# Spectral mix kernel: half of the modes' product is added to the stored x @ w_ch of 24 tiles, and the rest comes in pairs of tiles on 64-row quarters of TensorE

## The chip, the cores and the metric

The kernel runs on one core of one Trainium2 chip. The metric is the device time of one launch in microseconds (us), the median of several runs. Inputs and output are float32 in the chip's DRAM.

## The reference

Eight batches `b`, sequence `S` = 576, `DM` = 512 (8 heads of 64). First a sliding-window attention with a linear bias gives `x` (8 x 576 x 512). Then a spectral step keeps `NM` = 64 modes, and a channel product closes it:

```python
X = np.fft.rfft(x, axis=1)
Xr, Xi = np.real(X[:, :64]), np.imag(X[:, :64])
Yr = einsum('bmd,mde->bme', Xr, w_r) - einsum('bmd,mde->bme', Xi, w_i)
Yi = einsum('bmd,mde->bme', Xr, w_i) + einsum('bmd,mde->bme', Xi, w_r)
y = np.fft.irfft(Yr + 1j * Yi, n=576, axis=1)   # the other modes are zero
u = x + y
out = u + np.maximum(u @ w_ch, 0.0)
```

`w_r` and `w_i` are 64 x 512 x 512 each, 134 MB together, and are read once. Everything else is small beside them.

## The kernel before

The work has three stages.

**Attention** (to about 173 us of the span). It fills `x_sb` and `x4`, the tiles of `x`, and meanwhile a first quarter of the rows of the spectral weights is streamed and used.

**Streaming** (about 173 to 396 us). The other three quarters of the rows of `w_r` and `w_i` come through a ring of three buffers (`RING`), 1.5 MB at a time, two modes by `w_r` or by `w_i`. `_pair(g, m, w)` uses one such load in 24 matmuls (line 792), and `_send(g)` then issues the load that takes over its buffer. The loop runs over `i` from 0 to 59 (`NM - 4` = 60 steps), and the last four steps (60 to 63, with `BUSY` = 12 matmuls of filler after a step, line 709) come after it. The load of the last step is issued when step 60 has been used, in two halves. After every eighth mode the sums go to `ZT` (line 801), in four blocks of 16 modes (real and imaginary part: 32 rows each).

Into this loop other work is put, by the step at which it stands in the program:
- `_ft_steps` builds `FT`, the inverse transform, 128 rows of (mode, part) by 576 positions, for four orders of the mode blocks (one for `b % 4` each).
- `_xt` and `_xw(g, n, xT, psum)`: for each of 36 tiles of 128 positions (`g.seq`), `x` is transposed on TensorE and multiplied by `w_ch` (line 839, four matmuls, and one more where `g.way[n]` is "q", which adds `x`). The result is kept in `g.hl[:, n]` as a high and a low bf16 half: two copies on ScalarE (line 843), and two subtractions on VectorE (line 844), alternating. Its PSUM buffers are two.
- `_z_early(g, b, psum)`, for b = 0 to 7 in steps 50 to 57: of three mode blocks that are done, it makes `Z` (the spectrum, transposed to mode rows) and `ZW` (`Z @ w_ch`), 16 + 16 matmuls on 128 x 32 column strips, then one copy on VectorE and one on ScalarE.

At the end of the loop the PSUM buffers of `_xw` and `_z_early` are given to a new pool, `g.fps`, three `mm` and three `y` buffers, and `_known(g, i)` for the first three tiles is put in front of step 60.

**End** (`_finish`). The last mode block goes through `_z_late` (for four batches at a time) and `_z_take(g, b)`, which copies 32 rows of `ZW` and `Z` of one batch. Each of the 36 tiles needs two PSUM sums: `mm` = stored `x @ w_ch` + `FT.T @ ZW`, and `y` = `x` (for "a" tiles) + `FT.T @ Z`. `_halves` makes such a term as two matmuls that stand side by side, 128 rows deep and 64 columns wide each. Then an "a" tile takes ScalarE (relu of `mm`) and VectorE (add `y`), a "q" tile takes VectorE (max of `mm` and `x`), ScalarE (copy of `y`) and GpSimd (add). The store is issued by SyncE. Half of the 36 tiles are "q". The loop of `_finish` issues, for tile `i`, TensorE's work of `i`, the first step of `i - 1`, the add of `i - 2` and the late store of `i - 3`; the order on each engine is the order of the program.

Of the kernel before, what the change touches and what calls it, by code (L numbers as in the profile page):

```python
# [9 lines left out]
FP32 = mybir.dt.float32  # L10
# [6 lines left out]
P = 128  # L17
# [16 lines left out]
def kernel(  # L34
# [64 lines left out]
    g.X[-1] = persist.tile([P, len(GROUPS[-1]), 2, B, NM], BF16, name="Xlast")  # L99

    g.spectra = []
    g.seq = []
    for b in range(B):
        g.seq += [(g.x_sb[:, b, st], ((b, st * P), (b, st * P + 64))) for st in range(4)]
        if b % 2:
            g.seq.append((g.x4[:, b // 2], ((b - 1, 4 * P), (b, 4 * P))))
    g.way = ["q" if 2 <= i < len(g.seq) - 5 and i % 5 in (0, 2, 3) else "a" for i in range(len(g.seq))]

    with tc.manual_schedule(engines={ET.SP, ET.PE, ET.Activation, ET.DVE, ET.Pool}):
        with ExitStack() as wctx:  # L110
# [82 lines left out]
            with ExitStack() as xctx:  # L193
                xt = xctx.enter_context(tc.tile_pool(name="xts", bufs=2))
                xps = xctx.enter_context(
                    tc.tile_pool(name="xps", bufs=2, space=bass.MemoryType.PSUM))
                eps = xctx.enter_context(
                    tc.tile_pool(name="eps", bufs=1, space=bass.MemoryType.PSUM))
                ftq = _ft_steps(g, xt, xps)
                g.Xz = {}  # L200
                _expand(g, 0, xt, xps)
                k, xT = 0, None
                for i in range(NM - 4):
                    m, w = divmod(i, 2)
                    m *= 2
                    _pair(g, m, w)
                    _send(g)
                    if i % MB == 5:
                        _expand(g, m // MB + 1, xt, xps)
                    if i == 2 * RING - 1:  # L210
                        xT = _xt(g, 0, xt, xps)
                    while k < len(g.seq) and k * (NM - 4 - 2 * RING) < (i + 1 - 2 * RING) * len(g.seq):
                        nxt = _xt(g, k + 1, xt, xps) if k + 1 < len(g.seq) else None
                        _xw(g, k, xT, xps)
                        xT, k = nxt, k + 1
                    if i > 2 * RING and ftq:
                        ftq.pop(0)()
                    if 0 <= i - (NM - 14) < B:
                        _z_early(g, i - (NM - 14), eps)
            g.fps = ctx.enter_context(  # L220
                tc.tile_pool(name="fps", bufs=3, space=bass.MemoryType.PSUM))
            g.mm, g.y = {}, {}
            for i in range(3):
                _known(g, i)

            wps = mctx.enter_context(
                tc.tile_pool(name="wps", bufs=1, space=bass.MemoryType.PSUM))
# [82 lines left out]
    g.nc.scalar.activation(g.mask[:, h], g.rel, AF.Exp, scale=-(2.0 ** (-8.0 * (h + 1) / g.H)))  # L310


def _block(c, k):

    return 3 if k == c else c if k == 3 else k


def _ft_steps(g, pool, psum):
# [7 lines left out]
    def begin():  # L326
        box.cvec = pool.tile([P, 1], FP32, tag="cvec", name="cvec", bufs=1)
        nc.vector.memset(box.cvec, 2.0 / S)
        nc.vector.memset(box.cvec[0:1], 1.0 / S)
        nc.vector.memset(box.cvec[64:65], 1.0 / S)  # L330
        box.FTn = pool.tile([P, S], BF16, tag="FTn", name="FTn", bufs=1)
        for c in range(4):
            order = pool.tile([P, P], BF16, tag="order", name="order", bufs=4)
            for k in range(4):
                nc.gpsimd.tensor_copy(
                    order[:, 32 * k : 32 * k + 32].rearrange("p (r m) -> p r m", r=2),
                    src[:, _block(c, k)])
            orders.append(order)

    def natural(st):  # L340
# [489 lines left out]
def _xw(g, n, xT, psum):  # L830


    nc = g.nc
    x = g.seq[n][0]
    xw = psum.tile([P, g.DM], FP32, tag="xw", name="xw")
    if g.way[n] == "q":
        nc.tensor.matmul(xw, lhsT=g.ident_b, rhs=x, start=True, stop=False)
    for dt in range(4):
        nc.tensor.matmul(xw, lhsT=xT[:, dt], rhs=g.wch[:, dt],  # L839
                         start=(dt == 0 and g.way[n] != "q"), stop=(dt == 3))  # L840
    for h in range(2):
        hi, lo = slice(64 * h, 64 * h + 64), slice(64 - 64 * h, 128 - 64 * h)
        nc.scalar.copy(g.hl[hi, n, h], xw[hi])  # L843
        nc.vector.tensor_tensor(  # L844
            out=g.hl[lo, n, h], in0=xw[hi], in1=g.hl[hi, n, h], op=ALU.subtract)


def _z_early(g, b, psum):


    nc = g.nc
    zp = psum.tile([P, 4, P], FP32, tag="zp", name="zp")
    zwp = psum.tile([P, g.DM], FP32, tag="zwp", name="zwp")
    for et in range(4):
        for k in range(4):
            blk = _block(b % 4, k) % 3
            l = g.ZT[:, et, blk, :, b]
            ks = slice(32 * k, 32 * k + 32)
            nc.tensor.matmul(
                zwp[ks], lhsT=l, rhs=g.wch[:, et], start=(et == 0), stop=(et == 3),  # L860
                tile_position=(0, 32 * k))
            nc.tensor.matmul(
                zp[ks, et], lhsT=l, rhs=g.ident_b, start=True, stop=True,
                tile_position=(0, 32 * k))
    nc.vector.tensor_copy(g.Z[:, b], zp.rearrange("p a b -> p (a b)"))
    nc.scalar.copy(g.ZW[:, b], zwp)


def _z_late(g, b0, psum):
# [3 lines left out]
    zp = psum.tile([P, 4, P], FP32, tag="zp", name="zl")  # L873
    for et in range(4):
        for c in range(4):
            l = g.ZT[:, et, 3, :, b0 + c]
            nc.tensor.matmul(
                zwp[32 * c : 32 * c + 32], lhsT=l, rhs=g.wch[:, et],
                start=(et == 0), stop=(et == 3), tile_position=(0, 32 * c))
    for et in range(4):  # L880
        for c in range(4):
            l = g.ZT[:, et, 3, :, b0 + c]
            nc.tensor.matmul(
                zp[32 * c : 32 * c + 32, et], lhsT=l, rhs=g.ident_b, start=True, stop=True,
                tile_position=(0, 32 * c))
# [3 lines left out]
def _z_take(g, b):  # L889
    nc = g.nc  # L890
    zp, zwp = g.late
    ks = slice(32 * (b % 4), 32 * (b % 4) + 32)
    nc.scalar.copy(g.ZW[ks, b], zwp[ks])
    if b % 4 == 2:
        nc.scalar.copy(g.Z[ks, b], zp[ks])
# [1 line left out]
        nc.vector.tensor_copy(g.Z[ks, b], zp[ks])  # L897


def _known(g, i):  # L900

    nc = g.nc
    x = g.seq[i][0]
    g.mm[i] = g.fps.tile([P, g.DM], FP32, tag="mm", name="mm")
    g.y[i] = g.fps.tile([P, g.DM], FP32, tag="y", name="y")
    _halves(nc, g.mm[i], [g.ident2] * 2, [g.hl[:, i, h] for h in range(2)], start=True, stop=False)
    if g.way[i] == "a":
        _halves(nc, g.y[i], [g.ident_b[:, 0:64], g.ident_b[:, 64:128]], [x] * 2,
              start=True, stop=False)


def _finish(g):
# [5 lines left out]
    with ExitStack() as fctx:  # L918
        pool = fctx.enter_context(tc.tile_pool(name="fin", bufs=4))
        lps = fctx.enter_context(  # L920
            tc.tile_pool(name="lps", bufs=1, space=bass.MemoryType.PSUM, side="right"))
        first = [min(i for i, t in enumerate(g.seq) if t[1][0][0] == b and t[1][1][0] == b)
                 for b in range(g.B)]
        _z_late(g, 0, lps)
        _z_take(g, 0)
        o, r, y = {}, {}, {}
# [7 lines left out]

        for i in range(N + 3):
            if i < N:
                if i >= 3:
                    _known(g, i)
                ft = [g.FT[:, b % 4, s : s + 64] for b, s in g.seq[i][1]]
                _halves(nc, g.mm[i], ft, [g.ZW[:, b] for b, _ in g.seq[i][1]],  # L940
                      start=False, stop=True)
                _halves(nc, g.y[i], ft, [g.Z[:, b] for b, _ in g.seq[i][1]],
                      start=(g.way[i] == "q"), stop=True)
            if i == first[3] - 1:
                _z_late(g, 4, lps)
            for b in range(1, g.B):
                if i == first[b] - 3:
                    _z_take(g, b)
            j = i - 1
            if 0 <= j < N:  # L950
# [48 lines left out]
```

## Time and profile before

| what | value |
|---|---|
| median of 3 runs | 436.17 us (435.27 to 436.35) |
| the profiled execution: time, span of its instructions | 434.88 us, 433.1 us |
| mean granted TensorE clock | 0.837 |
| PE, DVE, ACT, POOL busy over the span | 73%, 54%, 49%, 24% |
| DMA rate over the span | 401 GB/s |
| last use of streamed weights starts | 395.22 us |
| first matmul of `_z_late` | 396.08 us |
| last matmuls of the last tile start | 427.09 us |
| last store lands | 432.03 us |

PE is TensorE, DVE is VectorE, ACT is ScalarE, POOL is GpSimd, SP is SyncE. All times in the text are microseconds from the first instruction of the span. An instruction that started at 398.47 and took 0.60 holds its result only at 399.07, but the next one on the same engine can start before that. The profiled execution is one run, 1.29 us below the median, so differences are worked out inside it and then set on the median.

### The profile page before, as it was taken

The numbers are of one execution on the slowest core, as the hardware profiler recorded it, in microseconds if no ns is written. First come the engines' busy times: TensorE is split into PE (matmuls) and PEld (weight loads), VectorE is DVE, ScalarE is ACT, GpSimd is POOL, SyncE is SP. The second block draws the span as 40 slices with busy tenths as digits, with TensorE's granted clock in tenths as the row PEclk, the third lists the DMA queues.
The fourth block names the chain that finished last, engine by engine and source line by source line (L and its number), as shares of the span: only waits on it lengthen the run. The fifth ranks groups of instructions, "written<-read, shape, count | busy, mean of one in ns | idle before, by whom it ended". The sixth has DMA issues, their size and how long they took to land.

```text
span 433.1 us, 11017 instructions
## 1 busy us (share of the span) xinstructions
PE 317.3 (73%) x4684; PEld 206.2 (48%) x4684; DVE 232.8 (54%) x425; ACT 212.4 (49%) x321; POOL 104.3 (24%) x160
## 2 busy tenths in 40 slices
PE   2688888898887787566857657766666579778994
PEld 1466666666666564433434333333333355544552
DVE  6478977777885473143343342433423445512884
ACT  4799969889887650022242322212313234302883
POOL 8766735445444102000000000000000000000983
PEclk9969999999999896557595885556956898989999
DMA  8999999999999999999999999999999999993787
GB/s 289 409 412 414 418 413 396 416 421 415 418 418 422 424 432 426 395 423 433 428 423 434 426 423 431 431 424 432 417 429 432 424 426 426 426 415 128 285 315 275
DMA packets 33664, 173.72 MB, mean 401 GB/s; under 512 B 3792, under 2 KB 3792, under 8 KB 21456
## 3 DMA queue, kind: packets, MB, share of 16 engines
q1 hardware_dynamic: 33616, 173.03, 97.1%
q8 instruction: 36, 0.59, 0.5%
q14 instruction: 12, 0.10, 0.1%
HBM read 163.58 MB, written 9.44 MB: 400 GB/s over the span
## 4 chain that ended last, share of the span: by engine, by line
DMA 58%; PE 22%; ACT 10%; DVE 6%; issue 2%; SPq 0%; ACTq 0%
DMA wring<-in_moe_w_r_dram 30%; DMA wring<-in_moe_w_i_dram 19%; PE acc L792 4%; ACT att L471 4%; DMA hl<-in_k_dram 3%; DMA hl<-in_q_dram 3%; PE mm L826 2%; DMA ZTa<-in_moe_w_r_dram 2%; PE av L496 2%; PE acc L758 2%; PE y L826 2%; PE xw L839 2%; ACT T L423 2%; DVE att L479 2%; DVE hl L844 1%
## 5 line engine op out<-in xcount | busy, mean ns | idle before, releaser
L843 ACT CAST hl<-xw 64x512 bf16<-64x512 f32 x72 | 41.7, 579 | 123.3 <-PE xw L839 87.2
L792 PE MATMUL acc<-Xz,wring 128*128 128x32 bf16 x1464 | 48.9, 183 | 62.4 <-DMA wring<-in_moe_w_i_dram 33.7
L792 PEld LDWEIGHTS <-wring 128*128 128x128 bf16 x1464 | 43.3, 101 | 94.8 <-DMA wring<-in_moe_w_i_dram 51.3
L844 DVE TENSOR_TENSOR hl<-xw,hl 64x512 bf16<-64x512 f32 x72 | 49.6, 689 | 69.6 <-ACT hl L843 67.5
L965 POOL TENSOR_TENSOR o<-r,ys 128x512 f32<-128x512 f32 x18 | 22.5, 1276 | 230.7 <-DVE r L957 229.3
L471 ACT ACTIVATE att<-sc 128x1024 bf16<-128x1024 f32 x64 | 66.2, 1035 | 19.5 <-PE sc L465 19.2
L479 DVE TENSOR_TENSOR att<-att,hl 128x1024 bf16<-128x1024 bf16 x64 | 54.7, 854 | 35.0 <-ACT att L471 34.6
L423 ACT COPY T<-tqk 128x512 bf16<-128x512 bf16 (+1 forms) x87 | 62.2, 758 | 4.2 <-PE tqk L413 3.6
L402 POOL CAST hl<-hl 128x576 bf16<-128x576 f32 x64 | 46.1, 748 | 45.2 <-issue 33.4
L839 PE MATMUL xw<-wch,xT 128*128 128x512 bf16 x144 | 55.2, 524 | 0.7 <-ACT FT L350 0.7
L413 PE MATMUL tqk<-ident_b,hl 128*128 128x128 bf16 x288 | 28.1, 239 | 10.0 <-POOL hl L402 6.4
L465 PE MATMUL sc<-T,T 64*128 64x256 bf16 (+2 forms) x320 | 26.6, 262 | 8.4 <-ACT att L471 7.1
L819 DVE COPY xT<-tp 128x512 bf16<-128x512 bf16 x36 | 15.2, 421 | 30.9 <-PE tp L817 30.6
L402 POOL CAST b<-hl 128x576 bf16<-128x576 f32 x32 | 25.0, 804 | 17.3 <-issue 8.0
L413 PEld LDWEIGHTS <-hl 128*128 128x128 bf16 x288 | 19.5, 106 | 19.1 <-issue 8.3
L839 PEld LDWEIGHTS <-xT 128*128 128x128 bf16 x144 | 17.6, 127 | 20.7 <-issue 16.2
L496 PE MATMUL av<-hl,att 128*128 128x65 bf16 (+1 forms) x576 | 23.8, 198 | 2.6 <-DVE hl L448 1.2
L514 DVE TENSOR_TENSOR x_sb<-av,rec 128x512 bf16<-128x512 f32 x32 | 22.1, 692 | 1.1
L496 PEld LDWEIGHTS <-att 128*128 128x128 bf16 (+1 forms) x576 | 20.0, 102 | 5.6 <-issue 1.6
L589 ACT CAST Xz<-xz 128x384 bf16<-128x384 f32 x16 | 7.7, 478 | 30.2 <-PE xz L583 29.8
L758 PE MATMUL acc<-wring 128*128 128x64 bf16 x480 | 18.9, 194 | 4.8 <-DMA wring<-in_moe_w_r_dram 2.2
L758 PEld LDWEIGHTS <-wring 128*128 128x128 bf16 x480 | 16.3, 99 | 6.0 <-DMA wring<-in_moe_w_r_dram 2.6
(114 smaller groups left out, 454.0 us busy)
## 6 DMA issues: line engine op xcount, KB each, us to landing
wring<-in_moe_w_i_dram SPq DMA_DIRECT2D x30, 1536.0 KB, 10.1
wring<-in_moe_w_r_dram SPq DMA_DIRECT2D x30, 1536.0 KB, 10.1
wring<-in_moe_w_r_dram SPq DMA_DIRECT2D x15, 1024.0 KB, 9.2
wring<-in_moe_w_i_dram SPq DMA_DIRECT2D x15, 1024.0 KB, 9.5
hl<-in_q_dram SPq DMA_DIRECT2D x32, 288.0 KB, 7.2
hl<-in_k_dram SPq DMA_DIRECT2D x32, 288.0 KB, 7.0
hl<-in_v_dram SPq DMA_DIRECT2D x32, 288.0 KB, 7.3
out_dram<-o SPq DMA_DIRECT2D x32, 256.0 KB, 2.9
```

The lines of the kernel that those rows point to most:

```text
L402: g.nc.gpsimd.tensor_copy(u.b[w][:, :, e], u.raw[w][e])
L413: g.nc.tensor.transpose(u.tp[:, r - r0], u.b[w][:, r].rearrange("p u d -> p (u d)"), g.ident_b)
L423: copy(u.T[w].rearrange("c h (p r) -> c (h p) r", r=g.R)[:, :, r0:r1], u.tp[:, 0 : r1 - r0].rearrange("c r p -> c p r"))
L465: nc.tensor.matmul(sc[:, e, c0 : c0 + nq], lhsT=kT[es, h, _start(kt) : _start(kt) + P], rhs=qT[es, h, kt * P : kt * P + nq], start=True, s ...
L471: nc.scalar.activation(a, sc, AF.Exp, scale=1.0 / math.sqrt(g.D))
L479: nc.vector.tensor_tensor(out=a, in0=a, in1=m, op=ALU.mult)
L496: nc.tensor.matmul(av[o, h, t * (D + 1) : (t + 1) * (D + 1)], lhsT=u.att[min(kt // 2, 1), h][:, f, c0 : c0 + m], rhs=vn[:, g.ST * h + kt, ...
L758: nc.tensor.matmul(acc[:, et, :, h : h + QUAD, :], lhsT=w[:, a].bitcast(BF16)[:, 1::2][:, et * P : (et + 1) * P], rhs=g.z0[:, a, 1 - k : 3 ...
L792: nc.tensor.matmul(acc[:, et, :, m - c0 : m - c0 + 2, :], lhsT=w[:, a].bitcast(BF16)[:, 1::2][:, et * P : (et + 1) * P], rhs=X[:, a, 1 - k ...
L839: nc.tensor.matmul(xw, lhsT=xT[:, dt], rhs=g.wch[:, dt], start=(dt == 0 and g.way[n] != "q"), stop=(dt == 3))
L843: nc.scalar.copy(g.hl[hi, n, h], xw[hi])
L844: nc.vector.tensor_tensor(out=g.hl[lo, n, h], in0=xw[hi], in1=g.hl[hi, n, h], op=ALU.subtract)
```

## The change

`FT` and `Z`/`ZW` get other orders of the mode blocks, so that for each batch the two blocks that are done first (modes 0 to 31) fill one half of the 128 rows, and the two late ones the other half; even and odd batches have them the other way round (`LAY`, `_half`). The tiles run by pairs of batches: of the nine tiles of a pair, six (places 1 to 6) are "folded".

- `_z_early` now makes modes 0 to 31 of two batches in one call (four calls, steps 32, 39, 46, 53), and `_z_mid`, new, makes modes 32 to 47 of four batches in one call (steps 49 and 53). They copy by 64 and by 32 rows: 16 copies each on VectorE and ScalarE, where there were 8.
- `_xw` of the 24 folded tiles gets one more matmul, 64 rows deep, that adds `FT.T @ ZW` of modes 0 to 31 to the stored sum. The 12 other tiles are made first, in steps 6 to 28, the folded ones in steps 33 to 59. Before, the 36 tiles were spread over steps 6 to 58.
- In `_finish`, the `mm` of two folded tiles (one of an even, one of an odd batch) get their remaining modes in `_late_mm`: four matmuls, 64 rows by 64 columns each, in place of four that were 128 rows by 64 columns. The `mm` sums of the two tiles are begun together.
- `_z_take` of batches 2 and 3 (and 6 and 7) stands behind tiles 5 and 6 (23 and 24), where it stood behind tiles 6 and 11 (24 and 29); the second `_z_late` behind tile 11 instead of 13.
- The number of "q" tiles stays 18. The first three tiles are "a", "q", "q", where they were "a", "a", "q".

```diff
+    for b in range(0, B, 2):
+        for c, st in ((0, 0), (0, 1), (1, 0), (0, 2), (1, 1), (0, 3), (1, 2), (1, 3)):
+            g.seq.append((g.x_sb[:, b + c, st], ((b + c, st * P), (b + c, st * P + 64))))
+        g.seq.append((g.x4[:, b // 2], ((b, 4 * P), (b + 1, 4 * P))))
+        g.way += "aqqaaqqaq" if b < B - 2 else "aqqaqaaaa"
+    g.pair = {i for i in range(len(g.seq)) if i % 9 in (1, 3, 5)}
+    g.fold = {i for i in range(len(g.seq)) if 1 <= i % 9 <= 6}
+    g.order = [i for i in range(len(g.seq)) if i not in g.fold] + sorted(g.fold)
...
+                for k in range(lone):
+                    jobs.append((2 * RING + 2 * k, _xw, k))
+                half = NM // 2
+                for c in range(0, B, 2):
+                    t = half + 7 * c // 2
+                    jobs.append((t, _z_early, c))
+                    jobs += [(t + 1 + k, _xw, lone + 3 * c + k) for k in range(6)]
+                jobs += [(half + MB * 2 + 1 + b, _z_mid, b) for b in range(0, B, 4)]
+                jobs.sort(key=lambda t: t[0])
...
+LAY = ((3, 2, 0, 1), (0, 1, 3, 2), (2, 3, 0, 1), (0, 1, 2, 3))
+LATE = tuple(o.index(3) for o in LAY)
+MID = tuple(o.index(2) for o in LAY)
+def _half(b):
+    return slice(64 * (b % 2), 64 * (b % 2) + 64)
...
 def _xw
     for dt in range(4):
         nc.tensor.matmul(xw, lhsT=xT[:, dt], rhs=g.wch[:, dt],
-                         start=(dt == 0 and g.way[n] != "q"), stop=(dt == 3))
+                         start=(dt == 0 and g.way[n] != "q"), stop=(dt == 3 and not fold))
+    if fold:
+        b, s = g.seq[n][1][0]
+        ks = _half(b + 1)
+        nc.tensor.matmul(xw, lhsT=g.FT[ks, b % 4, s : s + P], rhs=g.ZW[ks, b],
+                         start=False, stop=True, tile_position=(ks.start, 0))
...
+def _z_early(g, b0, psum):
+    _z_products(g, zp, zwp, [(k % 2, b0 + 1 - k // 2) for k in range(4)])
+    for b in (b0, b0 + 1):
+        ks = _half(b + 1)
+        nc.vector.tensor_copy(g.Z[ks, b], zp[ks].rearrange("p a b -> p (a b)"))
+        nc.scalar.copy(g.ZW[ks, b], zwp[ks])
+def _z_mid(g, b0, psum):
+    _z_products(g, zp, zwp, [(2, b0 + MID.index(k)) for k in range(4)])
+    for c in range(4):
+        ks = slice(32 * MID[c], 32 * MID[c] + 32)
+        nc.vector.tensor_copy(g.Z[ks, b0 + c], zp[ks].rearrange("p a b -> p (a b)"))
+        nc.scalar.copy(g.ZW[ks, b0 + c], zwp[ks])
...
+def _late_mm(g, i):
+    for h in range(2):
+        for n in (i, i + 1):
+            b, s = g.seq[n][1][h]
+            ks = _half(b)
+            nc.tensor.matmul(
+                g.mm[n][64 * h : 64 * h + 64], lhsT=g.FT[ks, b % 4, s : s + 64],
+                rhs=g.ZW[ks, b], start=False, stop=True, tile_position=(ks.start, 64 * h))
...
 def _finish
+                if i in g.pair:
+                    for n in (i, i + 1):
+                        if n >= 3:
+                            _known_mm(g, n)
+                    _late_mm(g, i)
+                elif i - 1 not in g.pair:
+                    if i >= 3:
+                        _known_mm(g, i)
+                    _halves(nc, g.mm[i], ft, [g.ZW[:, b] for b, _ in g.seq[i][1]],
+                          start=False, stop=True)
                 if i >= 3:
-                    _known(g, i)
+                    _known_y(g, i)
                 _halves(nc, g.y[i], ft, [g.Z[:, b] for b, _ in g.seq[i][1]],
                       start=(g.way[i] == "q"), stop=True)
-            if i == first[3] - 1:
+            if i == 11:
                 _z_late(g, 4, lps)
             for b in range(1, g.B):
-                if i == first[b] - 3:
+                if i == (9 * (b // 2) - 4 + b % 2 if b > 1 else 0):
                     _z_take(g, b)
```

## The prediction

> **What bounds the kernel now.** I read the page's slices first. Slices are 10.8 us.
>
> ```profile
> PE   2688888898887787566857657766666579778994
> PEclk9969999999999896557595885556956898989999
> DMA  8999999999999999999999999999999999993787
> DMA 58%; PE 22%; ACT 10%; DVE 6%; issue 2%; SPq 0%; ACTq 0%
> ```
>
> DMA is full until slice 36, and the chain agrees: to 395 us the weights' arrival sets the time. What the change puts into that stage costs nothing while TensorE and the copies keep ahead of the loads; only the hand-over and the end stage can move the time. Next, TensorE's timeline where one stage hands over to the other:
>
> ```profile
> 377.12 1.02 PE L839 MATMUL xw<-wch,xT 128*128 128x512 bf16 x4
> 380.82 0.82 PE L792 MATMUL acc<-Xz,wring 128*128 128x32 bf16 x24 [2.68 <-DMA wring<-in_moe_w_i_dram]
> 381.58 0.64 PE L826 MATMUL mm<-hl,ident 128*64 128x512 bf16 x2
> 384.30 0.78 PE L792 MATMUL acc<-Xz,wring 128*128 128x32 bf16 x24 [0.40 <-DMA wring<-in_moe_w_r_dram]
> 384.92 2.75 PE L709 MATMUL idle<-x_sb,ident_b 128*128 128x512 bf16 x12
> 387.94 0.77 PE L792 MATMUL acc<-Xz,wring 128*128 128x32 bf16 x24 [0.27 <-DMA wring<-in_moe_w_i_dram]
> ```
>
> The last `_xw` ran in step 58, and its copies were over before step 59 (380.82), so the first `_known` matmul waited for nothing. From step 60 on (384.30) TensorE is nearly full: a step and its filler take 0.62 + 12 x 0.2157 = 3.21 of the 3.64 between loads (0.2157 is the pitch of 512 columns at full clock: 12 matmuls end in 2.75, of which 0.38 is the last one alone). The end stage by windows:
>
> ```profile
> 400.00:405.00 5.00, 4.85 (x44) 2.90 (x42) 4.64 (x8) 4.59 (x9) 4.20 (x4) 1.00 0.61 233
> 405.00:410.00 5.00, 5.00 (x68) 3.04 (x66) 4.10 (x8) 3.25 (x8) 4.53 (x4) 1.00 0.83 289
> 415.00:420.00 5.00, 5.00 (x46) 3.12 (x45) 4.22 (x8) 4.21 (x9) 4.73 (x4) 1.00 0.92 318
> ```
>
> TensorE (first column after the length) is full, but VectorE, ScalarE and GpSimd stand at 3.3 to 4.7 of 5 too. There is no wide margin behind TensorE: a gain on it soon ends on the next engine.
>
> **Part by part. The streaming stage: nothing.** 24 folded matmuls add 24 x 0.2157 = 5.2 us of TensorE at full clock (10.4 at half); two calls fewer of the Z products take off 2 x 1.3 (a block of 32 takes 1.3 at 364.45); 8 + 8 more copies add 8 x 0.69 on VectorE and 8 x 0.585 on ScalarE. TensorE waited 62.4 us in this stage for loads (line 792's idle time). Steps 33 to 59 now hold about 0.6 + 0.2 + 5 or 6 x 0.22 = 2 us against 3.64. Step 53 has `_z_early` and `_z_mid` on one PSUM buffer: 1.3 + 1.4 (wait for the copies) + 1.3 + 1.9 = 6 us, 2.3 over its step, but two more loads are on their way then (10.1 from issue to landing), so 3.6 is free. If the cover were gone it would cost the 5.2.
>
> **The hand-over: +1.2.** The last `_xw` moves from step 58 to step 59, right ahead of `_known`, which takes the PSUM that `_xw`'s copies still read. Step 59 starts at 380.82, its 24 matmuls take 0.61, four pitches lead to the last of five `_xw` matmuls, with 0.1 for the change to 64 rows (below): 382.4. Its first copy starts 0.41 later (row: last `_xw` matmul at 377.77, copy at 378.18), and the chain copy, subtract, copy, subtract takes 2.63 (378.18 to 380.81): 385.5. Four `_known` passes (one fewer than before) and a change of shape: 0.96, so step 60 starts at 386.5, not 384.30. Queued behind that wait on TensorE are steps 60 to 63, on SP the last load, issued at 387.3 instead of 385.03; that one is free, since the queue is busy until 391.54 with the load ahead. Steps 60, 61 and the filler: 386.5 + 2 x 3.21, then 0.61 + 3 x 0.2157, then 0.30 + 5 x 0.2157 = 395.55 for the last use, against 395.22: **+0.35**. That is at full clock. TensorE now idles 2.7 us, from 382.8 to 385.5, and the clock can drop:
>
> ```profile
> 376.92:380.33 3.41, 1.23 (x19) 0.49 (x14) 2.28 (x4) 1.78 (x4) 0.00 (x0) 1.00 1.03 434
> 380.33:383.74 3.41, 2.92 (x34) 1.44 (x34) 0.94 (x2) 0.00 (x0) 0.00 (x0) 0.50 0.99 422
> ```
>
> The same gap of 2.68 us stood in the first of these stretches, and the next 3.41 us were at half clock (1.00, then 0.50 in the column after POOL). Before, that hit work which waited anyway. Now it would hit a queue without slack: up to half of 3.41 = +1.7. Since the stretches are 3.41 long and could fall anywhere, about half the places have the gap inside one stretch. I take 0.35 + 0.85 = 1.2; ends 0 and 2.1. The Trainium skill ("TensorE: Matmul & The Clock Gate", Part 1) says that the clock falls after a whole idle window of about 3.4 us; by that a gap of 2.7 would cost nothing and the hand-over be 0.35, but the two rows above show a drop after less.
>
> **TensorE's work in the end stage: about 0.** Of 126 passes (18 x 4 for "a", 18 x 3 for "q"), 5 were done ahead; 121 remain. Now 24 `mm` passes become 12, and 4 are done ahead: 110. That is 11 x 0.2157 = 2.4 saved, if four quarters run at once. The trace has no 64 x 64 tile, but its nearest rows are 64 rows deep:
>
> ```profile
> 101.13 0.64 PE L758 MATMUL acc<-wring 128*128 128x64 bf16 x16
> 101.70 0.39 PE L465 MATMUL sc<-T,T 64*128 64x256 bf16 x4
> 102.03 0.34 PE L413 MATMUL tqk<-ident_b,hl 128*128 128x128 bf16 x3
> ```
>
> Four of 256 columns in 0.39: one after another they would need 4 x 0.108 + 0.165 of drain = 0.60; two by two, 0.38. So halves by rows do run side by side, and halves by columns do in the end stage. But the rows also price the change of shape: 16 matmuls of 64 columns (0.029 apart) from 101.13 are through at 101.60, and the next shape starts at 101.70; from there 2 x 0.108 lead to 101.92, and the next starts at 102.03. About 0.1 each way. In the end stage itself:
>
> ```profile
> 406.94 0.41 PE L826 MATMUL y<-Z,FT 128*64 128x512 bf16 x2
> 407.28 1.09 PE L877 MATMUL zwl<-wch,ZTa 128*32 128x512 bf16 x16
> ```
>
> 0.34 where the pitch is 0.2157: 0.125. Each of 12 pairs enters and leaves quarters: 24 x 0.1 = 2.4 (2.3 to 3.0). Net 0 (-0.1 to +0.6).
>
> **Waits in the end stage: +1.0.** I followed the program's order with these pitches: TensorE 0.2157, VectorE 0.60, GpSimd 1.25, ScalarE 0.485, or 0.61 where the 32 rows of a take begin at another partition than the instruction beside it:
>
> ```profile
> 400.94 0.60 ACT L953 ACTIVATE r<-mm 128x512 f32<-128x512 f32 x1
> 401.56 0.58 ACT L893 CAST ZW<-zwl 32x512 bf16<-32x512 f32 x1
> 402.04 0.57 ACT L895 CAST Z<-zl 32x512 bf16<-32x512 f32 x1
> 402.64 0.58 ACT L956 COPY ys<-y 128x512 f32<-128x512 f32 x1
> ```
>
> For the kernel before, this puts the last tile's matmuls 31.0 after `_z_late`'s first, as the trace does (427.09 - 396.08), with 1.9 us of waits on TensorE after the first tile. For the changed one the waits add up to 2.9. A pair begins two `mm` at once, so its second needs a buffer one tile earlier: tile 4 waits 0.28 for the max of tile 1, and later pairs 0.21 twice. The takes of batches 2 and 3 now stand together, so ScalarE has relu of 3, two copies of batch 2, relu of 4, one copy of batch 3, then `ys` of 5: from 4.45 to 7.97 after `_z_late`. TensorE is done with tile 6 at 6.45, waits 0.33 for relu 4 (the `mm` of tile 7), and 0.79 for `ys` of 5 (its `y`). The same happens at tile 25. Behind these waits stand all later matmuls; who waits for them are VectorE and GpSimd, then the stores. The drain behind the last matmul stays the same (three tiles, last store split in two). Ends: 0.5 (the stores absorb half: from 416.58 to 431.71 they land 0.62 to 0.68 apart, so the queue is nearly full) and 1.5.
>
> Sum: 0 + 1.2 + 0 + 1.0 = +2.2; 434.88 + 2.2 = 437.1 for the profiled execution, 436.17 + 2.2 = 438.4 for the median, which lies 1.29 above it.
>
> **The rivals.**
> - *TensorE alone holds the end, and changes of shape are free* (faster). For it: TensorE full in the windows. Against: 0.1 in every row where the shape changes, and waits that don't fall with TensorE's work. Price: -2.4 + 0.35, at the waits of before: 434.1. It decides below 0.05 per change and with unchanged waits. The Trainium skill ("TensorEngine Tiling", Tiling Modes, Theoretical Speedup) has 64 x 64 as four independent tiles, up to 2 x for a dimension of 64, which would be this -2.4; its Key Properties also say that a change of mode drains TensorE, and that speaks against this change.
> - *Hidden*: clock holds, stores absorb the waits. 0.35 + 0.5 = +0.85: 437.0. The spacing of the stores speaks for it; against it, 2.0 us from issue to landing at the start and 2.85 at the end, so only 0.8 is queued.
> - *Quarters run two at a time*: 12 x 0.2157 = 2.6 back, partly under waits: 438.4 + 2 = 440.4. The rows at 101.70 speak against.
> - *The ring runs dry at step 53* (halves and copies slower than reckoned): up to 2 us more, 440.4. Against: 1.3 us of reserve there.
>
> **How the numbers follow.** Forecast 0.64, faster 0.08, hidden 0.17, two at a time 0.06, dry ring 0.05. 0.3% is 1.3 us, about what a measurement of this kernel can tell from no change, so "hidden" is the case within it: same 0.17, faster 0.08, slower 0.75. The range: low end 0.35 + 0 = 436.5 (clock holds, waits hidden), high end 2.1 + 0.6 + 1.5 = 440.4, rounded to 440.6 to take in the two worse rivals; "faster" stays outside.
>
> **What would show it.** Loads still landing 3.64 apart until step 59; `_known`'s first matmul at about 385.5 after a wait for VectorE's `hl`; step 60 about 2.2 late, half clock behind it or not; last use of weights 0.35 to 2 late. In the end stage, four quarter matmuls starting together, 0.1 of gap on either side, ScalarE's `ys` ending TensorE's waits at tiles 7 and 25. I am wrong if step 60 waits for its load alone, if the end stage (`_z_late` to last matmul) takes under 30.5 instead of 31 to 32.5, or if the ring's loads come apart.

## The result

The changed kernel's median is 440.8 us (438.43 to 444.96, six runs) against 435.86 us (434.69 to 437.1) for the kernel before, measured beside it: a ratio of 1.0122, 95% interval 1.0073 to 1.0171. It is slower by about 5 us. The forecast was 438.4 with a range to 440.6, so the sign was right and the size too small by more than half. The profiled execution took 440.48 us (span 438.7) where that of before took 434.88: 5.6 more.

The slices of the changed kernel, in the order of the prediction's first fence, with the rate of the DMA engines as the last row:

```profile
PE   2677888888888867445655655467578767779994
PEclk9989999999999995556755657599978999969998
DMA  8999999999999999999999999999999999992688
GB/s 284 410 412 415 416 400 413 418 416 420 418 419 421 416 432 427 415 428 426 426 425 428 429 428 428 420 413 425 427 426 392 427 428 361 426 403 81 251 301 289
```

The busy tenths still say that DMA is full until slice 36. The rate says otherwise in two places: 392 GB/s and 361 GB/s (the numbers 31 and 34 of the row), where the kernel before moved 432 and 426:

```profile
GB/s 289 409 412 414 418 413 396 416 421 415 418 418 422 424 432 426 395 423 433 428 423 434 426 423 431 431 424 432 417 429 432 424 426 426 426 415 128 285 315 275
```

A digit of 9 covers everything from 90% up, and these two dips hide under it. The hand-over, on TensorE's timeline:

```profile
382.58 0.77 PE L814 MATMUL acc<-Xz,wring 128*128 128x32 bf16 x24 [1.48 <-DMA wring<-in_moe_w_i_dram]
387.46 0.64 PE L848 MATMUL mm<-hl,ident 128*64 128x512 bf16 x2 [2.72 <-DVE hl L872]
389.31 0.82 PE L814 MATMUL acc<-Xz,wring 128*128 128x32 bf16 x24
399.76 1.09 PE L926 MATMUL zwl<-wch,ZTa 128*32 128x512 bf16 x16 [0.17 <-DVE ZTa L823]
```

And windows, the columns as in the prediction (the one after POOL is the granted clock); the first two answer to those shown of before, the other three are stretches of the clock around the 2.72 us gap (384.73 to 387.46):

```profile
400.00:405.00 5.00, 4.50 (x60) 2.24 (x54) 3.36 (x6) 3.53 (x7) 1.32 (x2) 1.00 0.01 2
405.00:410.00 5.00, 4.33 (x39) 2.24 (x36) 4.01 (x7) 4.56 (x9) 3.32 (x3) 1.00 0.68 263
380.81:384.22 3.41, 1.93 (x30) 0.98 (x29) 1.79 (x3) 1.16 (x2) 0.00 (x0) 1.00 1.01 429
384.22:387.63 3.41, 0.69 (x3) 0.20 (x5) 1.40 (x3) 1.16 (x2) 0.00 (x0) 0.50 1.03 434
387.63:391.04 3.41, 3.19 (x34) 1.45 (x34) 0.00 (x0) 0.00 (x0) 0.00 (x0) 0.50 0.99 422
```

The clock is at half from 384.22 to 391.04. It falls before the gap opens: the stretch ahead had TensorE busy for 1.93 of 3.41 us, with a wait of 1.48 for the load of step 59 in it. The gap leaves 0.69 of work in the next stretch, and the one behind that, in which most of the `_known` matmuls and step 60 run, is at half too.

TensorE stood at 4.85 and 5.00 in the first two windows before and stands at 4.50 and 4.33 now. `_z_late` starts 3.7 us later, so the windows see tiles some four or five places earlier: 0.42 of what the first one lacks is the wait for the first take, which the kernel before has ahead of its window. Of the 0.67 that the second lacks, 0.59 is one wait for `ys` at tile 7. So TensorE does wait; whether its work ends the stage, e3 below tells.

The landings, and the starts of the stages, divide the 5.6 us exactly:

| part of the profiled execution | before | after | more |
|---|---|---|---|
| first load behind the attention stage lands | 172.9 | 173.4 | 0.5 |
| from there to the last half load's landing | 222.3 | 224.1 | 1.8 |
| from that landing to the first matmul of `_z_late` | 0.91 | 2.29 | 1.4 |
| from that matmul to the last store's landing | 35.94 | 37.87 | 1.9 |

The first row moves by such an amount between executions (172.6 to 174.0 in those below), so it is no effect to explain. Inside the last row, from `_z_late`'s first matmul to the last tile's matmuls, 31.03 became 33.05.

**Where the loads came apart.** SPq is SyncE's queue issuing a load. Step 45's matmuls start at 329.03, and behind them stand:

```profile
329.87 0.54 SPq L695 DMA_DIRECT2D wring<-in_moe_w_r_dram  x1
331.83 0.81 PE L605 MATMUL xz<-Xlast,pick 128*128 128x192 bf16 x2 [1.34 <-DVE hl L872]
335.19 0.82 PE L814 MATMUL acc<-Xz,wring 128*128 128x32 bf16 x24
336.05 0.54 SPq L695 DMA_DIRECT2D wring<-in_moe_w_i_dram  x1
344.59 0.77 PE L814 MATMUL acc<-Xz,wring 128*128 128x32 bf16 x24 [2.06 <-DMA wring<-in_moe_w_i_dram]
```

And step 53, whose matmuls start at 359.22:

```profile
365.11 0.38 PE L884 MATMUL zwp<-wch,ZTa 128*32 128x512 bf16 x1 [1.28 <-ACT ZW L902]
366.64 0.78 PE L814 MATMUL acc<-Xz,wring 128*128 128x32 bf16 x24
```

Every eighth step (5, 13, up to 53) holds one more piece of work than the prediction counted: `_expand`, the `xz` matmuls of line 605, which lays out the spectrum for the next eight modes. Its tile shares the two PSUM buffers of `_xw`, so it waits for VectorE's copy of the tile before (1.34). Four `_xw` matmuls then take 1.81 where they take 1.03 at full clock. The step's successor starts at 335.19, and the load behind it is issued 6.18 after the one before instead of 3.64. In step 53 the two products of the change come on top of `_expand`. Most of that and the first product run at half clock (0.50 in the window 360.33 to 363.74), the second waits 1.28 for ScalarE's copy of the first, and the next issue comes 7.42 after the one before (360.03, then 367.45). The DMA view of these two issues, and of the punctual one at 360.03 (last number: us from issue to landing):

```profile
wring<-in_moe_w_i_dram SPq DMA_DIRECT2D x1, 1536.0 KB, 8.5
...
wring<-in_moe_w_i_dram SPq DMA_DIRECT2D x1, 1536.0 KB, 7.7
...
wring<-in_moe_w_r_dram SPq DMA_DIRECT2D x1, 1536.0 KB, 10.1
```

A load normally takes 10.1 because it queues behind others. The two late ones took 8.5 and 7.7, so their queue was short, and still they landed 4.83 and 5.01 after the load before them instead of 3.64. They came too late to keep the channel busy. This also gives a test for any late landing: with a time from issue to landing below 9.9 it was issued too late; above 10.3 something slowed the transfer itself; between the two it does not decide (e5 has one landing 4.67 apart after 10.2). Late landings of the second kind stand in every execution of both kernels (before: 4.48 apart near 358, after 11.27). What slows those is not known. They differ between executions, and here they make 2.4 us against 3.3 before; so the stage is only 1.8 us longer, though the two loads that were issued late make 2.56.

### The profile page after: what moved, and what is told of

Its sections match the earlier page's. It is cut to its first block, busy times and chain, and to the rows that moved or that the text cites. A ratio compares the mean times of both kernels' runs of the same rounds, so it can differ in the third digit from the quotient of the medians.

```text
span 438.7 us, 10915 instructions
## 1 busy us (share of the span) xinstructions
PE 310.4 (71%) x4618; PEld 197.3 (45%) x4644; DVE 238.7 (54%) x433; ACT 216.4 (49%) x329; POOL 103.8 (24%) x160
## 4 chain that ended last, share of the span: by engine, by line
DMA 54%; PE 22%; ACT 13%; DVE 7%; issue 2%; POOL 0%; ACTq 0%; SPq 0%; POOLq 0%; DVEq 0%
DMA wring<-in_moe_w_r_dram 34%; DMA wring<-in_moe_w_i_dram 20%; ACT att L493 6%; PE acc L814 4%; ACT T L445 3%; PE mm L848 2%; PE y L848 2%; PE idle L731 2%; PE acc L780 2%; PE sc L487 2%; DVE att L501 1%; PE xw L862 1%; DVE hl L872 1%; PE av L518 1%; DVE T L445 1%
## 5 line engine op out<-in xcount | busy, mean ns | idle before, releaser
L814 PEld LDWEIGHTS <-wring 128*128 128x128 bf16 x1464 | 42.9, 101 | 94.2 <-DMA wring<-in_moe_w_r_dram 49.6
L862 PE MATMUL xw<-wch,xT 128*128 128x512 bf16 x125 | 45.2, 477 | 3.3 <-issue 2.6
L862 PEld LDWEIGHTS <-xT 128*128 128x128 bf16 x144 | 16.1, 118 | 16.0 <-issue 9.0
L487 PEld LDWEIGHTS <-T 64*128 64x128 bf16 x320 | 12.4, 95 | 14.5 <-issue 8.1
## 6 DMA issues: line engine op xcount, KB each, us to landing
wring<-in_moe_w_i_dram SPq DMA_DIRECT2D x30, 1536.0 KB, 10.1
wring<-in_moe_w_r_dram SPq DMA_DIRECT2D x30, 1536.0 KB, 10.1
```

The lines of the kernel that those rows point to most:

```text
L487: nc.tensor.matmul(sc[:, e, c0 : c0 + nq], lhsT=kT[es, h, _start(kt) : _start(kt) + P], rhs=qT[es, h, kt * P : kt * P + nq], start=True, s ...
L814: nc.tensor.matmul(acc[:, et, :, m - c0 : m - c0 + 2, :], lhsT=w[:, a].bitcast(BF16)[:, 1::2][:, et * P : (et + 1) * P], rhs=X[:, a, 1 - k ...
L862: nc.tensor.matmul(xw, lhsT=xT[:, dt], rhs=g.wch[:, dt], start=(dt == 0 and g.way[n] != "q"), stop=(dt == 3 and not fold))
```

## The experiments

Theories: (A) the ring runs dry in the steps that hold `_expand`; (B) the hand-over's wait, with the half clock behind it, moves the end; (C) in the end stage, beginning two `mm` at once and the quarters cost more than the passes they save. Rivals: the late landings are chance; the hand-over is hidden; the end stage's loss is the order of takes and tiles. All ratios are to the kernel before on the same chip. "Late loads" is worked out from each load's issue and landing: what landings with a time below 9.9 stand over 3.64 apart, of those over 3.95 (all in us).

| kernel | median us | ratio, 95% interval | late loads | last landing to `_z_late` | `_z_late` to last matmuls | `_z_late` to last store |
|---|---|---|---|---|---|---|
| before | 435.86 | 1 | 0.3 | 0.91 | 31.03 | 35.94 |
| after | 440.8 | 1.0122 (1.0073 to 1.0171) | 2.6 | 2.29 | 33.05 | 37.87 |
| after_again | 440.9 | 1.0120 (1.0083 to 1.0156) | 1.7 | 2.00 | 33.03 | 37.82 |
| e1_known_late | 438.82 | 1.0087 (1.0067 to 1.0107) | 4.2 | 0.90 | 33.04 | 37.83 |
| e2_ring | 438.63 | 1.0082 (1.0063 to 1.0101) | 0 | 2.27 | 33.04 | 37.83 |
| e5_both | 437.06 | 1.0035 (1.0017 to 1.0053) | 0 | 0.91 | 33.03 | 37.79 |
| e7_filler | 440.0 | 1.0109 (1.0093 to 1.0124) | 2.0 | 1.25 | 33.04 | 37.99 |
| e3_unfold | 439.68 | 1.0099 (1.0082 to 1.0116) | 0.6 | 2.18 | 31.23 | 36.49 |
| e11_pairs_full | 440.64 | 1.0110 (1.0080 to 1.0140) | 2.1 | 2.92 | 32.22 | 37.44 |
| e8_folded_t1 | 437.72 | 1.0045 (1.0031 to 1.0059) | 0.6 | 0.90 | 33.21 | 38.07 |
| e10_unfold_both | 435.58 | 0.9989 (0.9971 to 1.0008) | 0 | 0.90 | 31.25 | 36.04 |
| e9_unfold_t4 | 434.64 | 0.9986 (0.9964 to 1.0008) | 0 | 0.90 | 29.75 | 35.23 |
| e13_all | 434.64 | 0.9979 (0.9962 to 0.9996) | 0 | 1.48 | 29.74 | 35.22 |
| e12_before_takes | 434.5 | 0.9985 (0.9965 to 1.0005) | 0 | 0.90 | 29.95 | 34.66 |

The four columns on the right come from one profiled execution each, which is not the median run. The length of the streaming stage (222.3 before, 224.1 after, from the first landing to the last) goes with the late loads: 222.3 to 223.1 in the nine traces with at most 0.6 us of them, 223.5 to 225.7 in the five with 1.7 or more. And in all six traces that keep the changed kernel's step 53 (after, after_again, e1, e3, e7, e11) the issue behind it comes 6.2 to 9.3 after the one before. So the late loads are not chance.

**after_again.** The changed kernel once more, with the second group of runs.

> The changed kernel itself, beside the other runs of this call on one chip. All theories: ratio 1.010 to 1.014 to the kernel before, the loads behind steps 45 and 53 over 1 us late at a time from issue to landing below 10 us, and 33.0 us from the last block's first product to the last matmul. If the late loads are chance (rival), they stand at other steps in this execution.

The same ratio. Step 53 again made its load late (4.90 apart after 8.4), while step 45 did not: there the next issue came 3.94 later. So step 53 is late in both executions, and step 45 is at the edge. A smaller delay of the same kind (4.09 apart after 9.0) stood eight steps earlier.

**e2_ring: the long steps are split.**

```diff
-                jobs += [(half + MB * 2 + 1 + b, _z_mid, b) for b in range(0, B, 4)]
+                jobs += [(49, _z_mid, 0), (56, _z_mid, 4)]
+                jobs = [(t + 1 if (t, job) == (45, _xw) else t, job, k) for t, job, k in jobs]
```

> The second product of modes 32 to 47 is moved from step 53 to step 56, and the x @ w_ch tile of step 45 (where the sums of eight modes are also transposed) to step 46. If the ring of loads runs dry because these two steps issue their successor's load too late (issues 6.2 and 7.4 us apart), the loads of these steps land at most 3.9 us after the one before instead of 4.83 and 5.01, and the time falls by 1.8 to 2.5 us, to a ratio of about 1.007. If the two late loads are hiccups of the transfers themselves, or the loads behind them make up for them (rival), gaps of 4.8 us stay or come elsewhere and the time stays within 0.5 us of the changed kernel, 1.012.

No load is late by its issue any more, and the time is at 1.0082. SyncE's queue around step 45:

```profile
333.83 0.54 SPq L696 DMA_DIRECT2D wring<-in_moe_w_i_dram  x1
338.90 0.54 SPq L696 DMA_DIRECT2D wring<-in_moe_w_r_dram  x1
```

The issue at 338.90 comes 5.07 after the one before, 1.43 late, and the load still landed 3.67 after its predecessor: that much the ring absorbs. The traces bear theory A out; the ratio alone does not part e2 from the changed kernel, whose interval begins at 1.0083, and e5 below decides. Two landings stay late (4.83 and 5.01 apart), but after 11.2 and 11.4 us from issue, which is the other kind.

**e1_known_late: the first tiles' stored sums behind step 60.**

```diff
-            for i in range(3):
-                _known_mm(g, i)
-                _known_y(g, i)
...
-                    _pair(g, m, w, BUSY)
+                    first = m == NM - 4 and w == 0
+                    _pair(g, m, w, BUSY - 4 if first else BUSY)
                     _send(g)
+                    if first:
+                        for i in range(3):
+                            _known_mm(g, i)
+                            _known_y(g, i)
```

> The stored sums of the first three tiles are put back into PSUM behind step 60 instead of in front of it (and that step has 4 filler matmuls less), so no load's use waits for the last copies of the x @ w_ch tile in step 59. If the wait at the hand-over costs what the two traces differ by there (2.26 us from the last landing to the first matmul of the last block's product, against 0.90), that distance is back at 0.9 to 1.1, the end stage stays at 33 us, and the time falls by 1.2 to 1.4 us, to a ratio of about 1.009 to the kernel before. If the hand-over is hidden by the loads (rival), the distance may shrink but the time stays within 0.4 us of the changed kernel, 1.012.

The distance is back at 0.90 and the ratio at 1.0087, as theory B has it. Here too the intervals overlap, and e5 decides whether the wait was hidden. In this profiled execution step 53 was worse than in the changed kernel: issues 359.52 and 368.84, and the landing 6.95 after the one before. Two windows of step 53 show why (clock in the column after POOL):

```profile
361.82:365.23 3.41, 2.34 (x34) 1.16 (x33) 1.33 (x3) 1.49 (x3) 0.00 (x0) 0.64 1.03 434
365.23:368.64 3.41, 3.21 (x56) 2.29 (x56) 0.91 (x2) 0.69 (x2) 0.00 (x0) 0.50 0.77 328
```

The clock was below full, and the second product (from 365.43) ran at half speed too. How late a long step gets depends on where the clock's stretches fall, and that differs between executions.

**e5_both: the two edits together.**

> The edits of e1 and e2 together; the end stage is the changed kernel's. If the dry ring and the hand-over are two separate costs that both set the end, the saved times add up: 1.8 + 1.3, so 3.1 us under the changed kernel, ratio about 1.005; the rest is the end stage's 2.0 us. If one hides the other (rival), it saves only as much as the larger, ratio 1.008.

1.0035, a little better than the 1.005 expected. From 1.0120 the ratio fell by 0.0033 with e1's edit alone, by 0.0038 with e2's, by 0.0085 with both: within the intervals they add up. The interval of e5 (1.0017 to 1.0053) lies wholly below that of e1 (from 1.0067) and that of e2 (from 1.0063), so each edit saves time beside the other: theories A and B hold, and neither cost hides the other. What remains is the end stage.

**e7_filler: the gap at the hand-over is filled.**

```diff
             wps = mctx.enter_context(
                 tc.tile_pool(name="wps", bufs=1, space=bass.MemoryType.PSUM))
             g.idle = wps.tile([P, DM], FP32)
+            _idle(g, 14)
             for i in range(3):
                 _known_mm(g, i)
```

(The pool is opened ahead of the stored sums instead of behind them.)

> 14 filler matmuls (of 0.22 us at full clock) stand in the gap on TensorE between the last x @ w_ch tile and the first stored sum that goes back into PSUM. If most of the loss at the hand-over is the half clock that follows the gap, the granted clock stays at 1.0 through steps 60 to 63 and the last landing to the first product matmul takes 1.2 to 1.5 us instead of 2.26, the time falls by 0.7 to 1.0 us, ratio 1.010. If the loss is the wait itself (rival), the distance stays at 2.0 to 2.4 and the time within 0.3 us of the changed kernel.

At the times of the two stretches that were at 0.50 in the changed kernel the clock is full, here the second:

```profile
387.63:391.04 3.41, 3.41 (x42) 1.84 (x42) 0.00 (x0) 0.00 (x0) 0.00 (x0) 1.00 1.01 432
```

The distance falls from 2.29 to 1.25, so at least 1.04 of the 1.4 us was the half clock. The other 0.34 is no clean measure of the wait, because the fillers last longer than the gap:

```profile
386.52 0.69 DVE L873 TENSOR_TENSOR hl<-xw,hl 64x512 bf16<-64x512 f32 x1 [0.65 <-ACT hl L872]
387.60 0.41 PE L849 MATMUL mm<-hl,ident 128*64 128x512 bf16 x2
```

The last `hl` is ready at 387.21, and the fillers hold TensorE until 387.60. In time the step is smaller than the intervals (1.0109 against 1.0120), so the split rests on the profiles: one with the gap filled, and five with it open (after, after_again, e2, e3, e11), in all of which the clock was at half for 6.8 us around it.

**e3_unfold: no folded matmul, no pairs, no quarters.** The schedule, the tiles' order, the takes and the ways of the changed kernel stay.

```diff
-    g.pair = {i for i in range(len(g.seq)) if i % 9 in (1, 3, 5)}
+    g.pair = set()
...
-                         start=(dt == 0 and g.way[n] != "q"), stop=(dt == 3 and not fold))
-    if fold:
+                         start=(dt == 0 and g.way[n] != "q"), stop=(dt == 3))
+    if False:
```

> Leaves out the folded matmul of the 24 tiles, and makes the mm of every tile with two 128-deep, 64-wide matmuls again, one tile at a time; schedule of the products, order of the tiles, takes and ways stay those of the changed kernel. If the quarters and the pairs of mm sums cost more than they save (shape changes of 0.244 us per pair against 0.197 saved, and buffers taken a tile early), the end stage (first matmul of the last block's product to last matmul) falls from 33.05 to 31.0 to 31.5, and the time by 1.5 to 2.3 us including 0.3 at the hand-over, to a ratio of about 1.007 to 1.009. If the end stage's loss is that of the order of takes and ways alone (rival), the end stage stays at 33 or gets longer by up to 2.4 us (11 passes more), and the ratio is 1.012 to 1.016.

The end stage falls to 31.23 with 11 passes more on TensorE, so passes did not set its end. The time fell by less than expected (1.0099): to the last store only 1.38 of the 1.82 us arrive.

**e11_pairs_full: pairs without quarters.** Like e3, but `_late_mm` stays, with full-depth halves:

```diff
-    for h in range(2):
-        for n in (i, i + 1):
+    for n in (i, i + 1):
+        for h in range(2):
             b, s = g.seq[n][1][h]
-            ks = _half(b)
             nc.tensor.matmul(
-                g.mm[n][64 * h : 64 * h + 64], lhsT=g.FT[ks, b % 4, s : s + 64],
-                rhs=g.ZW[ks, b], start=False, stop=True, tile_position=(ks.start, 64 * h))
+                g.mm[n][64 * h : 64 * h + 64], lhsT=g.FT[:, b % 4, s : s + 64],
+                rhs=g.ZW[:, b], start=False, stop=True, tile_position=(0, 64 * h))
```

> Like e3 (no folded matmul, full depth in the end), but the mm sums of two tiles are still begun together, with four 128-deep, 64-wide matmuls in place of the four quarters; so it has the pairs' hold on the buffers without the quarters. If the end stage's loss comes from beginning two mm at once, it takes 32.1 to 32.6 us (e3: 31.23; the changed kernel: 33.05). If it comes from the quarters and their shape changes, it stays at 31.2 to 31.6. If quarters save what they were counted to save (11 passes, 2.4 us), it is longer than the changed kernel's 33.05.

32.22, which divides the end stage: 31.03 before; +0.2 by the new order, ways and takes (31.23); +1.0 by beginning two `mm` at once (32.22); +0.8 by the quarters (33.05). The first expectation was met, but pairs are not the whole loss: quarters hold nearly as much. The largest wait that the profile lists (us in total, times, longest) is the same in all three kernels of the changed order; e11's:

```profile
PE y L848 <- ACT ys L1027: 1.2, 2, 0.6
```

The 1.0 us of the pairs is not in that list: it is short waits that hide in the modelled tail of the matmul before (0.38 to 0.41 long at a pitch of 0.2157). One of them, at tile 16 of e11's timeline:

```profile
416.06 0.38 PE L848 MATMUL mm<-ZW,FT 128*64 128x512 bf16 x2
416.53 0.41 PE L848 MATMUL y<-x_sb,ident_b 128*64 128x512 bf16 x2
```

The second line starts 0.47 after the first, a pitch and 0.25 of wait, and has no idle time beside it. They show when the start of each tile's `y` is set against e3's, counted from `_z_late`: 0.17 later at tile 4, 0.5 at tile 16, 0.8 at tile 25, 1.0 at tile 33. By the starts, 0.54 of it stands at the second `mm` of a pair (tiles 4, 22 and 31), 0.22 at the `mm` of tiles 7 and 25, and 0.25 at tile 16, behind two takes that stand together: those of batches 4 and 5 come behind tiles 14 and 15 in the changed kernel and behind 15 and 20 before, a move that the list of changes leaves out. The quarters' part, on the pair of tiles 12 and 13 of the changed kernel, where no buffer is waited for, and on the pair of tiles 5 and 6 of e11:

```profile
412.50 0.62 PE L848 MATMUL mm<-hl,ident 128*64 128x512 bf16 x4
413.05 0.41 PE L973 MATMUL mm<-ZW,FT 64*64 64x512 bf16 x4
413.39 0.41 PE L848 MATMUL y<-x_sb,ident_b 128*64 128x512 bf16 x2
```

```profile
405.46 0.62 PE L848 MATMUL mm<-hl,ident 128*64 128x512 bf16 x4
406.32 0.41 PE L848 MATMUL y<-Z,FT 128*64 128x512 bf16 x2
```

Four quarters at once save one pass of two, and the pair still takes 0.89 against 0.86 from its first matmul to the first `y`. The entry and exit take 0.12 each instead of the 0.1 reckoned, and the second pass behind them starts 0.24 after the first (413.39 to 413.63) instead of 0.2157. Nine pairs lose about 0.4 us together in this way, and three (from tiles 3, 21 and 30) lose 0.13 each, which makes the 0.8. In time e11 cannot be told from the changed kernel, and only 0.4 of the 0.8 us reaches its last store.

**e8_folded_t1: e5 with spread takes.**

```diff
-                if i == (9 * (b // 2) - 4 + b % 2 if b > 1 else 0):
+                if i == (0, 0, 1, 7, 13, 15, 17, 19)[b]:
```

> Like e5 (both streaming edits, folded tiles and quarters kept), with the takes of batches 2 to 7 behind tiles 1, 7, 13, 15, 17 and 19, so that no two of them stand together on ScalarE. If the bunched takes cost time in the changed kernel's end stage, it takes 32.2 to 32.5 us instead of 33.03, and the ratio goes from 1.0035 to about 1.002. If pairs and quarters alone hold the end stage, it stays at 32.9 to 33.1 and the ratio at 1.0035.

A miss: 33.21, and 1.0045. The wait moved and did not go:

```profile
PE mm L850 <- ACT r L1027: 1.3, 3, 0.7
```

The 1.2 us for `ys` are gone, and three waits for the relu, which frees the `mm` buffer, take 1.3. With two `mm` begun at once, wherever the takes stood here, an `mm` or a `y` was missing.

**e10_unfold_both, e9_unfold_t4 and e13_all: both streaming edits and no folding.** e10 has the changed kernel's takes; e9, and e13 for a narrower interval, have these:

```diff
-                if i == (9 * (b // 2) - 4 + b % 2 if b > 1 else 0):
+                if i == (0, 0, 5, 8, 14, 17, 23, 26)[b]:
```

> The edits of e1, e2 and e3 together, with the changed kernel's takes (e9 without its other takes). If the saved times add up, the end stage takes 31.2 us and the ratio is 1.000 to 1.002; against e9 (29.75 us, 0.9986) this is what the spread takes bring. If the end of the stores absorbs what the matmuls save (rival), the ratio is that of e9, 0.9986.

> The edits of e1, e2 and e3 together, and the takes of batches 2 to 7 behind tiles 5, 8, 14, 17, 23 and 26 (in the changed kernel 5, 6, 14, 15, 23, 24), so that two of them never stand together on ScalarE. What is left of the change is the early products by pairs of batches and the order of tiles. If waits for ScalarE behind bunched takes are what is left of the end stage's loss, it takes 29.6 to 30.2 us (31.03 before), the hand-over 0.9, and the ratio is 0.995 to 0.999. If the end stage is bounded by TensorE, with 121 passes as before, it stays at 31.0 to 31.3 and the ratio is 1.000.

> The kernel of e9 once more (both streaming edits, no folded matmul, spread takes), for a narrower interval: ratio 0.998 to 0.999, its end stage 29.7 to 29.8 us, if the first five rounds were typical.

e10 is back at the kernel before (0.9989, an interval that holds 1), and its interval lies wholly below that of e5, from which it differs by the folding alone; so theory C holds, and the three causes account for the whole loss. In e13 the distance at the hand-over is 1.48 although no `_known` matmul waits there: two stretches were at half clock (383.10 to 389.93), with no gap longer than 2.00. In e9's end stage the only wait on TensorE that is listed, beside `_z_late`'s first, is that for the first take:

```profile
PE mm L850 <- ACT ZW L944: 0.4, 1, 0.4
```

Its end stage falls from 31.25 to 29.75; of these 1.5 us, 0.8 reach the last store. In 24 runs of e9 and e13 the median was 434.64 both times; e13's interval, 0.9962 to 0.9996, lies just below 1, e9's holds it.

**e12_before_takes: the kernel before with other takes.**

```diff
-                if i == first[b] - 3:
+                if i == (0, 1, 5, 11, 14, 20, 24, 30)[b]:
```

> The kernel before, with its takes of batches 1 to 7 behind tiles 1, 5, 11, 14, 20, 24 and 30 in place of 2, 6, 11, 15, 20, 24 and 29, nothing else. Takes further from the ys copies of TensorE's next y should shorten the end stage from 31.0 to 30.1 to 30.5, and the time by 0.3 to 0.7 us, ratio 0.9985 to 0.9993; no change if the takes do not bound the end stage of before.

29.95 in the profile and 434.5 us; the interval still holds 1 (0.9965 to 1.0005). So spread takes shorten the end stage of the kernel before by 1.1 us as well, without anything of the change. In time e12, e9 and e13 cannot be told apart, and a gain over the kernel before is not shown for e12.

## Why the prediction was right or wrong

- **The streaming stage: nothing.** Wrong, and the step that failed. Profiled, it cost 1.8 us; undone alone (e2), the ratio fell by 0.0038, which is 1.7 us of 435.5, and beside e1's edit (e1 to e5) by 0.0052, which is 2.3. Three things failed in it. Its list of what stands in a step left out `_expand`, in 45 and 53. Its times were those of full clock, though the clock row that it quoted has fives and sixes there. Step 53 took 7.42 instead of 6: 0.63 for its 24 matmuls and 1.61 for `_expand` (1.9 counted for the rest of the step), 2.37 and 1.53 for the two products (1.3 each), 1.28 for the wait (1.4). And "3.6 is free" took two loads in flight for a whole load of reserve. The two late issues were 2.54 and 3.78 behind a spacing of 3.64, and their loads 1.19 and 1.37: the ring absorbed 1.35 and 2.4 (1.43 in e2 at no loss). The rival "the ring runs dry at step 53" was this case, with a chance of 0.05 and up to 2 us; that step 45 would be late too was not foreseen. What the prediction named as a sign of being wrong, that the ring's loads come apart, is what was seen.
- **The hand-over: +1.2.** Right in size: 1.4, of which at least 1.04 clock (0.85 predicted) and at most 0.34 wait (0.35), with VectorE's `hl` as the releaser. The first `_known` matmul was put at 385.5 and came at 387.46, but the loads ahead of it were 1.76 later than before (382.58 against 380.82), which leaves 0.2. The clock went another way than predicted: it fell at 384.22, ahead of the gap, after a stretch with 1.93 of 3.41 us of work, and the gap kept it at half for a second stretch; with the gap filled (e7) neither was at half. No stretch was wholly idle (the least work in one was 0.69), which goes against the Trainium skill's whole idle window of 3.4 us ("TensorE: Matmul & The Clock Gate", Part 1). That 0.85 came near is partly luck: a gap of 2.7 lies inside one stretch of 3.41 at a fifth of the places, not at half.
- **TensorE's work in the end stage: 0 (-0.1 to +0.6).** Wrong in size: +0.8. That four quarters run at once was right (they start within 0.01 us of each other), so "two at a time" is out. The change of shape was mis-sized: 0.12 each way and 0.02 on the next pass, beside 0.13 in all at each of three pairs.
- **Waits in the end stage: +1.0.** Right in size, 1.2 (0.2 and 1.0), and at the tiles named: tile 4, and `ys` at tiles 7 and 25 with 0.59 each in the list. But the listed waits of tiles 7 and 25 stand in e3 too, which takes only 0.2 longer than before; what costs is the pairs (e11 against e3): 0.54 at their second `mm`, which the prediction priced at 0.28 and twice 0.21, and the rest at tiles 7, 16 and 25. So the total was right partly by luck.
- **Faster, 0.08.** Its condition, changes of shape below 0.05, was not met. The rule of the Trainium skill cited beside it ("TensorEngine Tiling", Key Properties), that a change of mode drains TensorE, agrees with the 0.12 measured.
- **Hidden, 0.17.** Not met: 1.9 of the end stage's 2.0 us reach the last store. The spacing of the stores that spoke for it was misread: it runs from 0.31 to 0.99 in the stretch named, not from 0.62 to 0.68.

The sum by parts: 2.2 predicted; 0.2 more at the hand-over, 0.8 for the quarters, 0.2 for waits and 1.8 for the ring make 5.2, of which the end of the stores absorbs a little; 0.5 lies in the attention stage of that execution.

## What to carry to other kernels

A transfer-bound stage has slack only per step: for each step write down all that the program puts there, at the clock that the profile grants there, and compare the issue of the next load with what the queue can absorb, not with the sum of idle time. Work that is taken off an engine brings nothing when buffers, and not passes, set the order; look at the waits that stay in a kernel with the buffers of the new one. And after each stage, read the rate and the time from issue to landing beside a busy digit of 9.

## What the hardware showed

- In the changed kernel a load of 1.5 MB that was issued late to a draining queue took 7.7 and 8.5 us to land; with 3.64 per load, 4.1 to 4.9 us pass before its own transfer (an estimate from these numbers). In a ring of three buffers that lands one load each 3.64 us, an issue 1.4 us late cost nothing (e2), and one 2.5 us late cost 1.2. The limit is not one number: in e3 a load issued 2.56 late landed on time, and the one behind it 0.62 late.
- Four matmuls on quarters start within 0.01 us of each other, but going in and out costs 0.12 us each way: a pair of tiles with one group of quarters took 0.89 to its first `y`, one with two passes of halves 0.86.
- The clock fell to half behind a stretch of 3.41 us in which TensorE worked for 1.93, with no gap longer than 1.48 in it; a gap of 2.7 us then kept it at half, 6.8 us in all. With 14 filler matmuls in the gap it stayed at full, in the one execution profiled.
- A wait of 0.25 us behind a matmul of 512 columns was in no list of waits; it showed only as a start later than the pitch.
